# Diagonal squares of the first attention chunk, batched by head groups 0-1, 2-4 and 5-7 instead of 0-1, 2-3 and 4-7

## The chip, the cores and the metric

The kernel runs on one core of one Trainium2 chip. The metric is the time of one execution on the device in microseconds (us). The engines are named as in the profile: PE is the matmul engine (PEld its weight loads), DVE the vector engine, ACT the scalar engine, POOL the GpSimd engine, and SP the engine that issues most of the DMAs.

## What is computed

Two attention layers over 2048 tokens, with 640 channels in 32 heads of 20, whose outputs are laid side by side. Layer A works in four segments of 512 tokens: causal softmax attention inside the segment, mixed by a gate with a read from a memory that the earlier segments have written. Layer B is causal attention with a window of 256 tokens. Of the reference, cut down:

```python
for s in range(4):                       # layer A, segments of L = 512
    p = softmax(qs @ ks.T * scale + causal_mask)
    a_mem = (phi(qs) @ M) / (phi(qs) @ z + 1e-6)
    outs.append(g * a_mem + (1 - g) * (p @ vs))
    M, z = M + phi(ks).T @ vs, z + phi(ks).sum()
# layer B: p = softmax(q @ k.T * scale, where 0 <= i - j < 256);  p @ v
out = concat([A @ wo_A, B @ wo_B])
```

The change lies in segment 0 of layer A, where the memory is still empty.

## The kernel before

**Chunks and groups.** The work is cut into eight chunks of 512 tokens, A0, B0, A1, B1 and so on. The 32 heads form 8 groups of 4 heads. The projections of a chunk are done in five pieces of 128 channels (`qk_job`): piece m gives the q or k of group m (four heads of 20 rows, on partitions 0, 32, 64 and 96), and in the 12 left-over rows of each 32 a part of the heads of groups 5 to 7. Groups 5 to 7 are put together by DMA: when the last piece is there, `regroup` (line 429) stores the left-over rows to DRAM (four DMAs at line 436) and loads them back into place (four DMAs at line 444, one for each head of a group), for k and for q. So groups 0 to 4 can be scored as soon as their piece is done, and groups 5 to 7 only when these DMAs have landed.

**Score batches.** `batches` (line 1091) writes the list of score batches, in the order in which they are issued. For a chunk of A, a group has two strip batches (called a and b here, `BANKS_A`): the scores of 128 keys against all queries from the 65th of that key tile on. What is missing on the diagonal are squares of 64 queries by 64 keys, four for each group. They are batched over several groups, by `SQUARES0` for the first chunk and `SQUARES` for the others: `(g0, ng)` is a batch of the squares of groups g0 to g0 + ng - 1, put right behind the two strip batches of group g0. In this text A3a is the first strip batch of group 3, and S23 the batch of the squares of groups 2 and 3. `score_batch` (line 729) does a batch: its matmuls (line 741; 8 in a strip batch, 16 for each group in a squares batch) into two PSUM tiles `sc`, of which there are three in turn (`NSC`), two exponentials on ACT (line 757) that write two of ten `pt` tiles, and the masks: on POOL for strips (line 796), on DVE for squares (line 774).

**After the scores.** When all batches of a group are there, `av` (line 801) multiplies the `pt` tiles with v: 32 matmuls at line 810. It is called AV3 here for group 3. Then come a transpose on DVE (line 866), which frees the PSUM bank, the reciprocal (891) and the scaling on POOL (901). A `pt` tile is free again when AV of all groups in it has run. The squares take v from a second copy `vS`, which two DMAs for each half of the heads make from `vA` (line 684); its second half serves groups 4 to 7.

**What sets the order.** The kernel writes its instructions in one fixed order for each engine. The order comes from a planner in the kernel (`Flow`, line 63), which charges each piece of work with a written-in cost and puts next what its model says is ready. [...] When a batch is moved, the planner replaces everything behind it anew.

**Around the change** PE also has the projections of A0 (weights `wk_A`, `wq_A`, `wv_A`) and of B0 (`wBk`, `wBq`, `wBv`), all by the helper `wide` (line 853): 5 matmuls of 512 columns for a q or k piece, 5 of 320 columns for a tile of v. DVE evicts them (lines 484, 659 and 664). From each pair of k pieces of A0 come the features phi(k) (`phi`, line 495: ACT line 504, DVE lines 519 and 525); `phi_k` (line 565) stores each piece (`scr_pk`, line 578) and, after the fifth, loads all of them back by a transposing DMA (`pkT`, line 573). SP issues all of these DMAs in its one order. The regroup in `regroup`:

```python
self.nc.sync.dma_start(out=scratch[...], in_=dst[HD * j + DH:HD * j + HD, 0:self.KT, ...])   # line 436
...
self.nc.sync.dma_start(out=dst[HD * j:HD * j + DH, self.KT:G, ...], in_=scratch[...])        # line 444
```

Of the kernel before, what the change touches and what calls it, by code (L numbers as in the profile page):

```python
# [40 lines left out]
SH = P // 2  # L41
XC = SH + L

SQUARES = [(0, 4), (4, 4)]
SQUARES0 = [(0, 2), (2, 2), (4, 4)]
BANKS_A = [[(0, 0), (3, 448)], [(1, 0), (2, 320)]]

STRETCH = 10240.0 / 3.0
# [160 lines left out]
class _K:  # L209
# [881 lines left out]
    def batches(self, chunks):  # L1091

        out = []
        near = lambda n: ("near", 0, n)
        far = lambda n: ("far", P + SH, n)
        for n, (kind, c) in enumerate(chunks):
            if kind == "A":  # L1100
                for g0, ng in SQUARES0 if c == 0 else SQUARES:
                    for g in range(g0, g0 + ng):
                        for ent in BANKS_A:
                            out.append([n, [(g, ("a", kt), P * kt + SH, L - P * kt - SH, c0)
                                            for kt, c0 in ent], [("part", c0, SH) for _, c0 in ent], []])
                        if g == g0:
                            out.append([n, [(g0 + x, ("st"[kt % 2], kt), P * kt, SH,
                                             P * x + SH * (kt // 2))
                                            for x in range(ng) for kt in range(LT)],
                                        [("ends", 1, P * ng)], []])  # L1110
                        out[-1][3].append(g)
                continue

            def ends(g, qt, c0):
                return [(g, ("l", qt + 1), P * qt + SH, SH, c0),
                        (g, ("u", qt - 2), P * qt, SH, c0)]
            if n == len(chunks) - 1:
                for qt in range(LT):
                    for g0 in (0, 2, 4, 6):
                        ent = []  # L1120
                        for x in range(2):
                            ent += [(g0 + x, ("f", qt), P * qt, P, 256 * x),
                                    (g0 + x, ("f", qt - 1), P * qt, P, 256 * x + P)]
                        out.append([n, ent, [near(2), far(2)], []])
                        if g0 == 2:
                            out.append([n, [e for g in range(G) for e in ends(g, qt, SH * g)],
                                        [("ends", 0, L)], [(qt, 0)]])
                    out[-1][3].append((qt, 4))
                continue
            for g0 in range(0, G, 2):  # L1130
                for g in (g0, g0 + 1):
                    ent = [(g, ("f", 0), 0, 2 * P, 0), (g, ("f", 3), 3 * P, P, 2 * P)]
                    if c > 0:
                        ent.append((g, ("f", -1), 0, P, 3 * P))
                    out.append([n, ent, [near(2), far(2 if c else 1)], []])
                    out.append([n, [(g, ("f", 1), P, 2 * P, 0), (g, ("f", 2), 2 * P, 2 * P, 2 * P)],
                                [near(2), far(2)], []])
                    if g == g0:
                        out.append([n, [e for x in range(2) for qt in range(LT)
                                        for e in ends(g0 + x, qt, 256 * x + SH * qt)],  # L1140
                                    [("ends", 0, L)], [g0]])
                out[-1][3].append(g0 + 1)
        return out
# [433 lines left out]
```

## Time and profile before

| what | value |
|---|---|
| median of three runs | 336.32 us (334.82 to 336.74) |
| the profiled execution, its own time | 337.27 us |
| its span, first to last instruction | 335.5 us |
| mean granted clock of PE in it | 0.995 |
| PE busy, share of the span | 94% |
| ACT busy | 90% |
| DVE busy | 79% |
| POOL busy | 76% |

All views are of the profiled execution. The page gives busy shares of the whole span and of 40 equal slices of 8.4 us each. The timeline lists instructions by start time: start, duration, engine, line, operation, result and operands, shape, count, and in brackets the idle time before them with what ended it. The table by stretches gives the length, the busy time of each engine, the granted clock of PE (1.00 is full rate) and the busy share of the DMA engines. SPq is SP's queue of DMA issues.

### The profile page before, as it was taken

The numbers are of one execution on the slowest core, as the hardware profiler recorded it, in microseconds if no ns is written. First come the engines' busy times: TensorE is split into PE (matmuls) and PEld (weight loads), VectorE is DVE, ScalarE is ACT, GpSimd is POOL, SyncE is SP. The second block draws the span as 40 slices with busy tenths as digits, with TensorE's granted clock in tenths as the row PEclk, the third lists the DMA queues.
The fourth block names the chain that finished last, engine by engine and source line by source line (L and its number), as shares of the span: only waits on it lengthen the run. The fifth ranks groups of instructions, "written<-read, shape, count | busy, mean of one in ns | idle before, by whom it ended". The sixth has DMA issues, their size and how long they took to land.

```text
span 335.5 us, 15797 instructions
## 1 busy us (share of the span) xinstructions
PE 317.0 (94%) x6581; PEld 174.8 (52%) x6617; DVE 264.7 (79%) x555; ACT 303.3 (90%) x333; POOL 255.2 (76%) x648
## 2 busy tenths in 40 slices
PE   7899899999899999989999999999999999999996
PEld 2445355545554445455654445555554445666674
DVE  6878467689987899998877899997767889967553
ACT  2899589999899999999999999999999999999861
POOL 8466268898676979986875969997775979987850
PEclk9999799999999999999999999999999999999999
DMA  7966726674566655054598436133674045787862
GB/s 201 388 223 137 172 56 190 163 169 135 139 164 168 148 129 169 3 134 73 122 205 204 98 79 177 31 81 65 135 186 106 9 111 162 162 179 149 171 143 99
DMA packets 76260, 47.28 MB, mean 141 GB/s; under 512 B 48381, under 2 KB 73181, under 8 KB 76189
## 3 DMA queue, kind: packets, MB, share of 16 engines
q1 hardware_dynamic: 75325, 45.46, 55.3%
q8 instruction: 51, 0.84, 1.1%
q10 hardware_dynamic: 864, 0.82, 0.8%
q14 instruction: 20, 0.16, 0.2%
HBM read 17.62 MB, written 16.96 MB: 103 GB/s over the span
## 4 chain that ended last, share of the span: by engine, by line
PE 59%; DVE 16%; POOL 9%; ACT 7%; issue 4%; DMA 2%; SPq 2%; DVEq 0%; ACTq 0%; POOLq 0%
PE m L853 37%; PE sc L741 11%; PE m L810 7%; ACT pt L757 7%; POOL pt L796 5%; DVE pt L774 3%; DVE tt L866 3%; PE m L831 2%; POOL u L901 2%; DMA beta<-in_A_beta_dram 1%; DVE vA L659 1%; DVE kA L484 1%; POOL o L901 1%; SPq L444 1%; DVE pq L525 1%
## 5 line engine op out<-in xcount | busy, mean ns | idle before, releaser
L757 ACT ACTIVATE pt<-sc 128x1024 bf16<-128x1024 f32 (+2 forms) x306 | 285.0, 1013 | 15.8 <-PE sc L741 13.8
L796 POOL TENSOR_SCALAR_AFFINE_SELECT pt<-pt 128x128 bf16<-128x128 bf16 (+1 forms) x512 | 176.3, 372 | 65.8 <-ACT pt L757 61.1
L866 DVE STREAM_TRANSPOSE tt<-m 128x512 f32<-128x512 f32 x88 | 61.3, 710 | 22.7 <-PE m L810 11.0
L901 POOL TENSOR_TENSOR o<-tt,rr 128x320 bf16<-128x320 f32 x64 | 47.7, 746 | 4.2 <-DVE rr L891 4.2
L853 PEld LDWEIGHTS <-xT 128*128 128x128 bf16 x350 | 32.0, 97 | 24.2 <-issue 12.1
L741 PE MATMUL sc<-qB,kB 20*64 20x64 bf16 (+2 forms) x1728 | 38.4, 218 | 0.6 <-ACT pt L757 0.2
L774 DVE TENSOR_TENSOR pt<-pt,ends 128x1024 bf16<-128x1024 bf16 (+1 forms) x50 | 36.0, 734 | 0.0
L741 PE MATMUL sc<-qA,kA 20*64 20x64 bf16 (+4 forms) x1024 | 34.2, 238 | 1.9 <-DMA qA<-scr_qA 1.1
L741 PEld LDWEIGHTS <-kB 20*64 20x64 bf16 (+1 forms) x1728 | 21.6, 98 | 22.3 <-issue 20.8
L1010 DVE CAST ot<-m 128x320 bf16<-128x320 f32 x56 | 26.8, 485 | 7.5 <-PE m L853 7.3
L853 PEld LDWEIGHTS <-oT 128*128 128x128 bf16 x280 | 24.7, 97 | 11.8 <-issue 1.5
L853 PE MATMUL m<-wBv,xT 128*128 128x320 bf16 x160 | 26.9, 300 | 2.4 <-DVE tt L866 2.3
L853 PE MATMUL m<-wv_A,xT 128*128 128x320 bf16 x160 | 26.0, 300 | 2.4 <-DVE vA L659 1.7
L853 PE MATMUL m<-xT,wBq 128*128 128x512 bf16 x94 | 26.8, 391 | 0.9 <-DVE tt L866 0.4
L853 PE MATMUL m<-xT,wBk 128*128 128x512 bf16 x86 | 25.9, 388 | 0.7
L853 PE MATMUL m<-xT,wk_A 128*128 128x512 bf16 x94 | 25.2, 387 | 1.3 <-DVE qA L484 0.7
L853 PE MATMUL m<-xT,wq_A 128*128 128x512 bf16 x90 | 25.0, 381 | 1.3 <-DVE vA L659 0.9
L741 PEld LDWEIGHTS <-kA 20*128 20x128 bf16 (+1 forms) x1024 | 14.0, 97 | 23.4 <-issue 22.5
L810 PE MATMUL m<-pt,vA 128*32 128x192 bf16 (+3 forms) x512 | 23.6, 276 | 0.0
L853 PE MATMUL m<-wo_A,oT 128*128 128x320 bf16 x140 | 22.8, 300 | 0.4 <-DVE vA L659 0.3
L484 DVE CAST kB<-m 128x512 bf16<-128x512 f32 x20 | 13.8, 692 | 9.5 <-PE m L853 9.3
L484 DVE CAST qB<-m 128x512 bf16<-128x512 f32 x20 | 13.8, 689 | 7.7 <-PE m L853 7.7
(107 smaller groups left out, 412.5 us busy)
## 6 DMA issues: line engine op xcount, KB each, us to landing
scr_o<-o SPq DMA_DIRECT2D x28, 160.0 KB
out_dram<-ot SPq DMA_DIRECT2D x28, 160.0 KB
xT<-in_B_x_dram SPq DMA_DIRECT2D x8, 288.0 KB
xT<-in_A_x_dram SPq DMA_DIRECT2D x8, 256.0 KB
scr_pk<-e SPq DMA_DIRECT2D x15, 128.0 KB
scr_kA<-kA SPq DMA_DIRECT2D x16, 60.0 KB
scr_qA<-qA SPq DMA_DIRECT2D x16, 60.0 KB
kA<-scr_kA SPq DMA_DIRECT2D x16, 60.0 KB
```

Source lines behind the costliest of these rows:

```text
L444: self.nc.sync.dma_start(out=dst[HD * j:HD * j + DH, self.KT:G, at:at + L], in_=scratch[:, :].rearrange("(g j d) s -> j d g s", j=4, d=DH)[j])
L484: nc.vector.tensor_copy(out=dst[:, m, at:at + L], in_=ps[:, :])
L741: nc.tensor.matmul(ps[j // 2][h0:h1, j % 2, c0:c0 + nq], lhsT=k[rows, g, k0:k0 + h1 - h0], rhs=q[rows, g, q0:q0 + nq], start=True, stop=Tr ...
L757: nc.scalar.activation(out=pt[:, :, lo:hi], in_=ps[i][:, :, lo:hi], func=ACT.Exp, scale=self.scale)
L774: nc.vector.tensor_tensor(out=blk, in0=blk, in1=self.ends[:, c0, :].unsqueeze(1).unsqueeze(1) .to_broadcast([P, 2, n // SH, SH]), op=ALU.mult)
L796: nc.gpsimd.affine_select(out=blk, in_=blk, pattern=pat, compare_op=ALU.is_ge, fill=self.zero, base=base, channel_multiplier=mul)
L810: nc.tensor.matmul(O[HD * j:HD * j + HD, q0:q0 + nq], lhsT=v[:, VS * h:VS * h + HD], rhs=pts[j // 2][:, j % 2, c0:c0 + nq], start=(n_ == 0 ...
L831: nc.tensor.matmul(O[HD * j:HD * j + HD, o0:o0 + nq], lhsT=v[:, VS * h:VS * h + HD], rhs=pts[j // 2][:, j % 2, c0:c0 + nq], start=(n_ == 0 ...
L853: self.nc.tensor.matmul(ps[:, 0:n], lhsT=lhsT, rhs=rhs, start=start, stop=stop)
L866: self.nc.vector.transpose(out=tt[:], in_=O[:, :])
L901: nc.gpsimd.tensor_tensor(out=to[:] if add_to else to, in0=a, in1=b, op=ALU.mult)
L1010: nc.vector.tensor_copy(out=ot[:, 320 * hf:320 * hf + 320], in_=ps[:, 0:320])
```

## The change

The tuple of a squares batch gets a third number, `at`, which says behind the strips of which of its groups the batch is put. It is 0 everywhere, so each batch still stands behind the strips of its first group. The batches of the first chunk become groups 0-1, 2-4 and 5-7. Those of the other chunks stay.

```diff
-SQUARES = [(0, 4), (4, 4)]
-SQUARES0 = [(0, 2), (2, 2), (4, 4)]
+SQUARES = [(0, 4, 0), (4, 4, 0)]
+SQUARES0 = [(0, 2, 0), (2, 3, 0), (5, 3, 0)]
...
-                for g0, ng in SQUARES0 if c == 0 else SQUARES:
+                for g0, ng, at in SQUARES0 if c == 0 else SQUARES:
                     for g in range(g0, g0 + ng):
...
-                        if g == g0:
+                        if g == g0 + at:
                             out.append([n, [(g0 + x, ("st"[kt % 2], kt), P * kt, SH,
                                              P * x + SH * (kt // 2))
                                             for x in range(ng) for kt in range(LT)],
                                         [("ends", 1, P * ng)], []])
-                        out[-1][3].append(g)
+                        if g >= g0 + at:
+                            out[-1][3].extend(range(g0 if g == g0 + at else g, g + 1))
```

The list of batches in the first chunk was A0a A0b S01 A1a A1b A2a A2b S23 A3a A3b A4a A4b S4567 A5a A5b A6a A6b A7a A7b. It becomes A0a A0b S01 A1a A1b A2a A2b S234 A3a A3b A4a A4b A5a A5b S567 A6a A6b A7a A7b. The orders of the two kernels are the same on each engine up to S23 or S234, and again from the first score batches of B0 on (some 57 us into the profiled execution); only `pt` tile numbers differ there. On PE, in order, with the number of matmuls:

```
before, from the fourth wBk matmul on:
wBk 4, S23 32, wBk 1, wBq 3, A3a 8, wBq 2, wv_A 5, A3b 8, AV2, wv_A 5, A4a 8, wv_A 10, A4b 8, AV3,
wBk 5, S4567 64, wBq 5, wBk 2, A5a 8, wBk 3, wBq 4, A5b 8, wBq 1, wBv 10, AV4, A6a 8, AV5, wBv 5,
A6b 8, wBv 5, wBk 4, A7a 8, wBk 1, wBq 5, wBk 1, A7b 8, wBk 4, AV6
after:
wBk 5, S234 48, wBq 5, A3a 8, wv_A 10, A3b 8, wv_A 5, AV2, A4a 8, wv_A 5, wBk 4, A4b 8, wBk 1, AV3,
A5a 8, wBq 5, wBk 3, A5b 8, wBk 2, wBq 5, wBv 5, AV4, S567 48, wBv 8, A6a 8, wBv 7, wBk 2,
A6b 8, wBk 3, AV5, A7a 8, wBq 5, wBk 2, A7b 8, wBk 3, AV6
```

On SP the fifth `scr_pk` store stands ahead of the four loads of k at line 444, no longer between those of k and those of q. The first part of the x of A1 (line 291), which stood right behind the loads of q, now stands behind the transposing load and the two `vS` DMAs. On DVE the two operations of the fifth phi(k) piece (lines 519 and 525) stand ahead of the eviction of the first q piece of B0 and of both masks of S234; before, line 525 stood behind both masks of S23, that eviction and one of `vA`.

## Prediction

> **What bounds the kernel now.** I read the page's first part (PE 94%, ACT 90%), then the slices for the places where both engines pause. There is one after the start, at slices 4 and 5:
>
> ```profile
> PE   7899899999899999989999999999999999999996
> ACT  2899589999899999999999999999999999999861
> PEclk9999799999999999999999999999999999999999
> ```
>
> Slice 5 (33.5 to 42 us) holds ACT at five tenths and the only dip of PE's clock. Elsewhere ACT runs almost without a gap, so a microsecond won or lost here goes to the end. The timeline of PE shows what happens:
>
> ```profile
> 32.61 1.25 PE L853 MATMUL m<-xT,wBk 128*128 128x512 bf16 x4
> 33.80 0.27 PE L741 MATMUL sc<-qA,kA 20*64 20x64 bf16 x16
> 34.58 0.44 PE L741 MATMUL sc<-qA,kA 20*64 20x64 bf16 x2 [0.51 <-DMA qA<-scr_qA]
> 35.39 0.18 PE L741 MATMUL sc<-qA,kA 20*64 20x64 bf16 x1 [0.37 <-DMA qA<-scr_qA]
> 35.80 0.55 PE L741 MATMUL sc<-qA,kA 20*64 20x64 bf16 x45 [0.23 <-DMA qA<-scr_qA]
> ```
>
> S4567 starts at 33.80 with the 16 matmuls of group 4, and those of group 5 wait for the four loads of q until 35.80. The table by stretches, cut where the clock changes, shows the price of that pause:
>
> ```profile
> 32.98:36.39 3.41, 2.17 (x69) 1.21 (x68) 1.42 (x3) 1.34 (x2) 1.91 (x6) 1.00 0.54 162
> 36.39:39.80 3.41, 3.19 (x14) 0.90 (x13) 1.22 (x3) 1.94 (x2) 0.00 (x0) 0.50 0.89 178
> 39.80:43.21 3.41, 3.31 (x31) 1.52 (x24) 2.34 (x5) 3.16 (x4) 1.22 (x5) 1.00 0.72 173
> ```
>
> For 3.41 us behind the pause the granted clock is 0.50. ACT has nothing meanwhile:
>
> ```profile
> 36.40 1.94 ACT L757 ACTIVATE pt<-sc 128x1024 bf16<-128x1024 f32 x2 [2.08 <-PE sc L741]
> 40.05 3.88 ACT L757 ACTIVATE pt<-sc 128x1024 bf16<-128x1024 f32 x4 [1.71 <-PE sc L741]
> 45.26 14.31 ACT L757 ACTIVATE pt<-sc 128x1024 bf16<-128x1024 f32 x16 [1.33 <-PE sc L741]
> ```
>
> From 45.26 on ACT is the bound: sixteen exponentials without a gap. So the question is when A6a's exponential, the one at 45.26, can start. The chain of waits says what the pause waits for, SP's queue:
>
> ```profile
> 31.77 0.36 SPq L578
> ...
> 32.23 0.30 SPq L444
> ...
> 33.36 2.40 DMA qA<-scr_qA
> ```
>
> The last load of q is issued at 33.36 and is there at 35.76.
>
> **Work added or removed: none.** The squares of groups 2 to 7 are 96 matmuls either way. ACT had two exponentials of 512 columns (0.594 us) and two of 1024 (1.031): 3.25 us. It gets four of 768, which last 0.815 in B0: 3.26. The DVE masks have no row for 768 columns; they lie between 0.42 (512) and 0.68 (1024), and I take the middle, so that four cost what the two pairs did. Only places move.
>
> **Ahead of the pause.** PE's projections are the same before the first matmul that needs a load (10 wBk, 5 wBq, 20 wv_A), so are four strip batches, AV2 and AV3. S234 has 16 matmuls more than S23 (0.26 us for 32, so 0.13 more), and the 16 of group 4 at 33.80 are gone from the pause. I carried the after order forward from 24.2 us with the rows' durations: 0.216 us for each 512-column matmul, 0.156 for 320 columns, 0.33 for a strip batch, 0.67 for AV, an eviction of 0.69 or 0.49. S234's exponentials are 0.22 longer each and start 0.2 later, so ACT's A4b ends at about 35.3 instead of 34.3; its slack was the 2.08 us of idle time. PE reaches A5a at 33.7 (no more waiting for banks than before) to 34.1, and finds q absent as S4567 did.
>
> **The landing.** SP now issues the fifth pk store ahead of k's four loads. It waits for DVE's line 525. That ran at 28.42 to 28.96 behind two masks and two evictions; now it stands right behind the eviction of the first k piece of B0 (25.82 to 26.51), so I put its end at 27.2. SP gets to it at 28.96 as its queue stands, so it costs no wait, k's loads move by 0.46 us, and q's loads keep their place at 32.23. Landing: 35.8, taken unchanged (35.4 if the store, out of the way earlier, frees the rings; 36.2 if k's shift is passed on). Behind q the transposing load comes at 33.80 instead of 35.73, because its last store is now three microseconds older, and `vS` at 36.9 instead of 38.80.
>
> **The clock.** The stretch at half rate is worth: from the end of S4567 (36.35) to the start of A5a (39.33 to 39.39) lie 7 wide matmuls and a gap of 0.22; at full rate 7 x 0.216 = 1.5. So 1.5 us are lost. What was streamed in the stretch before it? By the planner's own count (columns / 2.4, squares at half): wBk from 32.98 to 33.80, 0.83 us; S4567, 512 / 2.4 = 0.21; the first wBq, 0.04. [...] After: the same stretch holds A4b (0.21), the last wBk (0.21), AV3 (1280 / 2.4 = 0.53), A5a (0.21) and wBq from 36.05 (0.34): 1.50, a share of 0.44 if PE arrives at 34.0. If it arrives at 33.7 the poorest position of a stretch (32.4 to 35.8) holds 0.28. So the pause is as long, but what lies beside it is denser: AV3 and two strips stand where five projections and late squares stood. I take it that the clock holds, with the other case kept as a rival, since one row of the trace gives the bound from one side only: the next poorest stretch I found without a drop, 145.62 to 149.03, had PE busy for 2.49 us against 2.17.
>
> [...]
>
> **Behind the pause.** At full rate: A5a 35.8 to 36.05, wBq 5 and wBk 3 (1.73) to 37.8, A5b to 38.1, wBk 2 and wBq 5 (1.51) to 39.6, wBv 5 to 40.4, AV4 to 41.1, S567 (0.5) to 41.6, wBv 8 to 42.7 or 42.9, A6a to 43.2. A6a's exponential follows after 0.2 to 0.45 (0.45 in the trace): 43.4 to 43.65, with S567's done at 43.3. From there ACT has the same 8 exponentials to B0 and is fed in time (A6b 45.0, A7a 46.7, A7b 48.6). Against 45.26 that is 1.6 to 1.85 earlier. Of it 1.5 is the clock. The rest, 0.1 to 0.35, is that wBv 10 stood in a piece ahead of AV4 while ACT had nothing, and that a part of S4567's exponential (group 4) was done ahead of the pause, in S234. If the clock drops as before, the same count with eight matmuls at 0.43 gives A6a's exponential at 45.05: 0.2 earlier.
>
> **Sum** against the profiled execution (span 335.5, its own time 337.27): -1.4 for the clock (1.5, less what the later exponentials of A4b eat) and -0.2 for the order, -1.6. Nothing behind 57 us moves but in time, and ACT's gapless run carries it to the end. That execution is 0.95 above the median of 336.32; the difference is taken to carry over. **Forecast: 334.7 us**, about what the quickest of the three runs had (334.82), which may be one without the drop.
>
> **Rivals.**
>
> *The half-rate stretch stays* (chance 0.30). For it: the pause is as long, and an arrival at 33.7 makes a stretch of 0.28. Against it: the share at 34.0 is 0.44. The time is 336.3 - 0.2 = 336.1.
>
> *AV4 waits for vS* (0.13). AV4 comes at 40.4 instead of 43.75. `vS` was issued at 38.80 to 40.10; at q's pace (2.4 us) it lands at 42.5 there. If SP's transposing load does not move up (it waits for the slowest pk store), vS comes at 42.5 again and the gain is returned: PE stands 1.5 to 2 us, ACT with it, as S567 and A6a need `pt` tiles that only AV4 frees. The time is 336.4. Against it: the pk store is issued three microseconds earlier.
>
> *Slower: SP stands at the fifth pk store* (0.10). Before, k's loads did not depend on DVE's fifth phi piece; now they and q's do. From an end of line 525 later than 28.96 each microsecond delays the landing by one. If that operation ends at 31 (DVE's first phi operations or ACT's exponential come late), the landing is at 37.8: PE stands 3.8 us, the clock surely drops, and the time is 336.3 + 2.0 - 0.2 = 338.1.
>
> *The change does nothing that can be told* belongs to the second: the squares are 0.5 us of ACT that only change sides.
>
> **How the numbers follow.** Forecast 0.46, half rate 0.30, vS 0.13, SP 0.10, and 0.01 left. The forecast's own range is 333.6 (landing at 35.4, nothing waits) to 335.6 (landing at 36.2, A6a's exponential late). The range over all cases: down to 333.6, up to 337.2, which holds the first three and leaves most of the last out. A measurement tells about 0.5% (1.7 us) from no change; the forecast lies at -0.48%, so its chance is split nearly in halves. Faster by more 0.29, within 0.59 (the other half and the two rivals in the middle), slower 0.12 (SP's wait, and a late landing with a drop).
>
> **What would show it.** The stretch behind the pause at a granted clock of 1.00; the first waiting matmul is A5a, with its last wait ended at 35.4 to 36.2; ACT's idle time ahead of A5a down from 2.08 to some 0.9, and one idle time of about 1.5 ahead of S567; A6a's exponential at 43.4 to 43.7; the transposing load issued near 33.8. It is wrong if SP stands at line 578 behind DVE, if AV4 waits for vS, or if the clock shows 0.50 again.

## The result, and the profile after

| | before | changed |
|---|---|---|
| median | 336.53 us (4 runs, 334.82 to 337.59) | 340.75 us (4 runs, 340.11 to 341.22) |
| profiled execution | 337.27 us | 341.08 us |
| its span | 335.5 us | 339.4 us |

The ratio is 1.0129, with a 95% interval of 1.0082 to 1.0176: the change made the kernel slower by 1.3%, outside the range forecast and on the other side. (All ratios here leave out executions over 1.5% above the quickest of their kernel, so a ratio can differ from that of two medians.)

The page of the changed kernel, second part, shows where. The slices are 8.5 us now:

```profile
PE   8999399999999999989999999999999999999996
ACT  2899359999999999999999999989999999999961
PEclk9999699999999999999999999999999999999999
```

The one slice that had ACT at five tenths before has three, the next one five, and PE itself is at three tenths. The timeline of PE has the reason:

```profile
33.24 0.59 PE L810 MATMUL m<-pt,vA 128*32 128x448 bf16 x12
33.66 0.20 PE L810 MATMUL m<-pt,vS 128*32 128x64 bf16 x3
39.58 0.63 PE L810 MATMUL m<-pt,vS 128*32 128x64 bf16 x13 [5.72 <-DMA vS<-vA]
39.98 0.29 PE L810 MATMUL m<-pt,vA 128*32 128x64 bf16 x4
40.20 0.61 PE L741 MATMUL sc<-qA,kA 20*128 20x448 bf16 x8
```

This is AV3. Three of its 16 matmuls on squares run, and the fourth waits 5.72 us for a DMA into `vS`. Only then comes A5a (40.20), and no wait for q, for which S4567 had waited, is listed ahead of it. SP's part of the timeline says which DMA:

```profile
28.42 1.18 SPq L578 DMA_DIRECT2D scr_pk<-e  x2
29.66 1.72 SPq L444 DMA_DIRECT2D kA<-scr_kA  x4
31.47 2.40 SPq L444 DMA_DIRECT2D qA<-scr_qA  x4
33.92 2.54 SPq L573 DMA_TRANSPOSE pkT<-scr_pk  x1
36.57 1.31 SPq L684 DMA_DIRECT2D vS<-vA  x2
```

The only `vS` DMAs under way are those of the second half, groups 4 to 7. They are issued from 36.57 on, behind the transposing load, and the second one lands at 39.83. Group 3 belongs to the first half, whose copy was made long before. In the kernel before AV3 ran at 31.94, and these DMAs were issued at 38.80: it did not wait for them.

The table by stretches, cut where the clock changes (the granted clock is the figure behind the five engines), shows the second half of the price:

```profile
33.57:36.98 3.41, 0.29 (x15) 0.11 (x3) 0.47 (x1) 1.47 (x2) 1.57 (x6) 1.00 0.73 163
36.98:40.39 3.41, 0.76 (x21) 0.48 (x25) 0.08 (x1) 0.00 (x0) 0.00 (x0) 0.50 1.01 238
40.39:43.81 3.42, 3.20 (x15) 1.03 (x8) 1.58 (x3) 1.94 (x2) 1.77 (x5) 0.50 0.30 103
43.81:47.22 3.41, 3.31 (x34) 1.46 (x36) 1.79 (x3) 1.94 (x2) 1.09 (x4) 1.00 0.00 0
```

PE is at half rate for two stretches (6.83 us at 0.50). In the first it stands almost all the time and loses little; in the second it works. ACT's timeline gives the sum:

```profile
40.93 1.94 ACT L757 ACTIVATE pt<-sc 128x1024 bf16<-128x1024 f32 x2 [5.89 <-PE sc L741]
44.58 1.94 ACT L757 ACTIVATE pt<-sc 128x1024 bf16<-128x1024 f32 x2 [1.71 <-PE sc L741]
48.25 1.51 ACT L757 ACTIVATE pt<-sc 128x768 bf16<-128x768 f32 x2 [1.73 <-PE sc L741]
50.09 12.54 ACT L757 ACTIVATE pt<-sc 128x1024 bf16<-128x1024 f32 x14 [0.33 <-PE m L853]
```

A6a's exponential starts at 50.09, against 45.26 before: 4.8 us late. The span ends 3.9 late; where the 0.9 between is given back was not traced.

**Theory 1.** AV3 waits for data that it does not use. `av` reads 32 columns of weights for each head, though a head has 21 (`VS`). For the fourth head of group 3 (number 15) these are columns 315 to 346 of `vS`. The second half's DMAs write from column 336 on. The two overlap in 11 columns, whose products land in rows that nobody reads. That fits the row above, in which the fourth matmul is the one that waits. By this theory AV3 waits for the DMAs whenever they stand ahead of it in the program, whatever the data are needed for. Before, A4b alone stood between the last piece of wv_A, from which `vS` is copied, and AV3, and the planner wrote AV3 first. In the changed kernel four wBk matmuls, A4b and one more wBk stand there, by then the modelled time of the DMAs has come, and they are written first. **Rival 2:** `vS` is late because SP issues the transposing load ahead of it, and the wait would only move to another place. **Rival 3:** the regroup of q is what sets the time.

### The profile page after: what moved, and what is told of

Its sections match the earlier page's. It is cut to its first block, busy times and chain, and to the rows that moved or that the text cites. A ratio compares the mean times of both kernels' runs of the same rounds, so it can differ in the third digit from the quotient of the medians.

```text
span 339.4 us, 15791 instructions
## 1 busy us (share of the span) xinstructions
PE 316.9 (93%) x6580; PEld 174.7 (51%) x6617; DVE 264.0 (78%) x555; ACT 303.0 (89%) x333; POOL 255.8 (75%) x648
## 4 chain that ended last, share of the span: by engine, by line
PE 57%; DVE 16%; POOL 8%; ACT 7%; issue 5%; SPq 3%; DMA 3%; DVEq 0%; POOLq 0%; ACTq 0%
PE m L853 36%; PE sc L741 11%; PE m L810 7%; ACT pt L757 7%; POOL pt L796 5%; DVE tt L866 3%; DVE pt L774 3%; PE m L831 2%; DVE kA L484 2%; POOL u L901 2%; DMA beta<-in_A_beta_dram 1%; DVE pq L525 1%; SPq L444 1%; DVE pq L519 1%; DVE ot L1010 1%
## 5 line engine op out<-in xcount | busy, mean ns | idle before, releaser
L774 DVE TENSOR_TENSOR pt<-pt,ends 128x1024 bf16<-128x1024 bf16 (+2 forms) x50 | 35.6, 725 | 0.0
L741 PE MATMUL sc<-qA,kA 20*64 20x64 bf16 (+4 forms) x1024 | 33.4, 238 | 0.5
L853 PE MATMUL m<-wo_B,oT 128*128 128x320 bf16 x120 | 19.6, 300 | 0.3 <-DVE ot L1010 0.3
```

What stands on the lines that cost most here:

```text
L741: nc.tensor.matmul(ps[j // 2][h0:h1, j % 2, c0:c0 + nq], lhsT=k[rows, g, k0:k0 + h1 - h0], rhs=q[rows, g, q0:q0 + nq], start=True, stop=Tr ...
L774: nc.vector.tensor_tensor(out=blk, in0=blk, in1=self.ends[:, c0, :].unsqueeze(1).unsqueeze(1) .to_broadcast([P, 2, n // SH, SH]), op=ALU.mult)
L853: self.nc.tensor.matmul(ps[:, 0:n], lhsT=lhsT, rhs=rhs, start=start, stop=stop)
```

## The experiments

**The DMAs behind AV3 in the program** (`e1_hold`). All engines, SP among them, keep the order of the changed kernel:

```diff
+        if n == 0 and half == 1:
+            f.blocked.append((t, self.known("av3"), lambda t0: go()))
+        else:
+            f.at(t, go)          # in v_squares
...
+            if n == 0 and g == 3:
+                self.mark(f.pe - 200.0, "av3")
             O, bi = self.av(     # in one_group
```

> The changed kernel, with the two DMAs of the second vS half written into the program behind AV3 instead of ahead of it, and the order of the instructions on each engine unchanged (SP's too): only the wait of AV3's fourth square matmul on these DMAs goes. Theory 1 (AV3 waits for data that it does not use: its fourth head reads 32 columns of vS, 315 to 346, and the DMAs write from 336 on): the wait of 5.72 us in AV3 is gone, PE passes to A5a and waits there for q until 35.5 to 36.2, vS (issued at 36.6, landed at 39.8) is there before AV4 needs it, and the time is 334.5 to 336.5. Rival 2 (vS is late because SP issues the transposing load ahead of it, and groups 4 to 7 need it anyway): the wait moves to AV4 or A5a, and the time stays at 339 to 341. Rival 3 (the regroup of q lands late): A5a waits beyond 38, and the time stays above 338.5.

Measured: 1.0001 of before (0.9968 to 1.0035); 12 runs from 335.33 to 340.80, with a median of 339.05 beside 337.91 for before on the same chip. That is above the 334.5 to 336.5 expected, in part because before was higher here too (336.53 in the first measurement). PE's timeline of its profiled execution (335.33 us, span 333.6; the lines of the code stand 3 lower):

```profile
33.70 0.29 PE L813 MATMUL m<-pt,vS 128*32 128x64 bf16 x16
33.81 0.20 PE L813 MATMUL m<-pt,vA 128*32 128x64 bf16 x4
34.81 0.49 PE L744 MATMUL sc<-qA,kA 20*128 20x448 bf16 x2 [0.79 <-DMA qA<-scr_qA]
35.66 0.48 PE L744 MATMUL sc<-qA,kA 20*128 20x448 bf16 x6 [0.36 <-DMA qA<-scr_qA]
36.07 1.25 PE L856 MATMUL m<-xT,wBq 128*128 128x512 bf16 x4
```

The 16 matmuls run through, and A5a waits for q, as the prediction had it. `vS` is issued as late as in the changed kernel (36.81), yet AV4, which needs it, runs at 40.70 without a wait. The stretch behind the pause has the full clock:

```profile
36.39:39.80 3.41, 3.36 (x23) 1.36 (x23) 1.38 (x2) 3.18 (x4) 1.38 (x7) 1.00 0.99 206
```

So the wait makes the loss, or nearly all of it: with the same order on every engine and without the wait, the ratio tells no loss, though up to 0.35% stays possible, and the median is 1.1 us above before's. `vS` comes as late as before and A5a has its q at 35.66, so rival 2 falls as the cause, and so does rival 3.

**The same kernel once more** (`e8_hold_again`).

> A second look at the changed kernel with the second vS half behind AV3. Its twelve times spread over 335.3 to 340.8, while its profile (span 333.6) had the full clock throughout. If the spread comes from the time at which q lands and from the half clock behind it, a profile in the upper half shows q later than 36.5 and a clock of 0.50 behind it, and one in the lower half neither; AV3 waits for vS in neither.

One run, 336.67 us, span 333.8: the full clock again, A5a's q there at about 36.2, no wait in AV3. It fell in the lower half of the spread and showed what was expected of that half. For the upper half the mean granted clock of the twelve executions of `e1_hold` has the answer: the five from 335.33 to 337.62 us have 1.00, the three from 338.84 to 339.52 have 0.995, the mean of the profile of before, which has 3.41 us at 0.50, and the four from 340.26 on have 0.99, that of the changed kernel's, which has 6.83 us. That q was late in those is not recorded.

**`vS` as two tiles** (`e2_split` for the changed kernel, `e3_before_split` for the one before). The overlap itself is gone:

```diff
-        self.vS = big.tile([P, LT, VW], BF16, name="vS")
+        self.vS = [big.tile([P, LT, VW - 16 * VS], BF16, name="vS%d" % i) for i in range(2)]
...
-                return self.vS[:, 2 * (u % 2) + u // 2, :]
+                return self.vS[g // 4][:, 2 * (u % 2) + u // 2, :]
```

> The changed kernel with vS as two tiles, one for each half of the heads, each with its own 12 spare columns; the order on each engine is unchanged but for one more memset on POOL. AV3 of no chunk can wait for the second half. Theory 1: as the kernel with the DMAs behind AV3, within 0.5 us, or up to 0.5 us less since AV3 of A1 waits for it too in all the other kernels: 334.0 to 336.5. Rival 2: 339 to 341.

> The kernel before with vS as two tiles. Here AV3 of A0 stands ahead of the DMAs in the program and never waited for them. Theory 1: 336.0 to 336.6, at most 0.5 us less than before (AV3 of A1). The difference between this and the changed kernel with two tiles is what the change itself is worth; by the prediction -0.2 to -1.6 us, by a rival in which the change is bad of itself +1 us or more.

Measured: 1.0001 (0.9972 to 1.0031) for the changed kernel, 0.9989 (0.9962 to 1.0015) for the one before, on one chip. A second way to remove the wait gives the same as the first, and the kernel before, which had no wait, gains nothing that can be told. That the loss is there on this chip too when the wait stays is shown by `e4_vs_first` below. It also follows that AV3 of A1, which stands behind such DMAs in both kernels, costs nothing: the profiles of both list no wait there. The median of the first (338.52, beside 337.91 of before) lies above the 334.0 to 336.5 expected, and so does that of the second (337.88, expected 336.0 to 336.6): on this chip all of them ran higher. The profiled execution of `e2_split` is a long one (340.60) and shows one way to such a time:

```profile
34.53 0.20 PE L810 MATMUL m<-pt,vA 128*32 128x64 bf16 x4
36.72 1.74 PE L741 MATMUL sc<-qA,kA 20*128 20x448 bf16 x8 [1.98 <-DMA qA<-scr_qA]
38.40 0.61 PE L853 MATMUL m<-xT,wBq 128*128 128x512 bf16 x1
```

AV3 does not wait, but SP issues q's loads from 34.28 on instead of 31.47, A5a gets its last q near 38.2, and the clock is at 0.50 from 36.45 to 43.27. The pause ahead of A5a is 3.5 us long here and 1.7 in `e1_hold`, with the same order of work. But the length alone does not decide: the clock fell 1.7 us after PE had stopped (34.73), when the pause was about as long as the whole of that in `e1_hold`.

The places of the falls tell more. The clock is at 0.50 from 36.39 to 39.80 in the kernel before, from 36.98 to 43.81 in the changed one and from 36.45 to 43.27 in `e2_split`: for 3.41, 6.83 and 6.82 us. In the 3.41 us ahead of its fall (32.98 to 36.39) the kernel before had PE busy for 2.17 us; in the same 3.41 us `e1_hold` had PE busy for 2.25, and its clock held. `e3_before_split` has the same order on PE as the kernel before and as long a pause (33.88 to 35.87), but there the clock held, in the 3.41 us that end inside the pause and in those that begin there:

```profile
31.43:34.84 3.41, 2.72 (x64) 1.32 (x63) 2.21 (x5) 2.97 (x4) 2.59 (x9) 1.00 0.60 170
34.84:38.25 3.41, 2.70 (x61) 1.35 (x61) 0.62 (x2) 1.79 (x2) 0.87 (x2) 1.00 1.07 229
```

Ahead of the fall in `e2_split` PE was busy for 1.74 of 3.50 us (33.00 to 36.50). PE's busy time does not tell the two cases apart, for `e7_split_q_first` had PE busy for 1.91 of 3.50 us (34.00 to 37.50), a smaller share than the 2.17 of 3.41 ahead of the fall in the kernel before, and its clock held. Why the clock fell in one execution and held in another of the same order is not shown.

The mean clocks of all executions say that the changed order is not the safer one once its wait is gone. On this chip 7 of 24 executions of `e1_hold` and `e2_split` had the full clock and 8 had 0.99 or less; of before and `e3_before_split` 21 of 41 had the full clock and one had 0.99.

**The transposing load behind `vS`** (`e4_vs_first`). The wait stays, SP's order is changed:

```diff
-        gate = self.known("dm", c - 1) if c > 0 else (lambda: 0.0)
+        gate = self.known("dm", c - 1) if c > 0 else self.known("vS")   # set when vS is issued
...
```

> The changed kernel with the transposing load behind the second vS pair on SP instead of ahead of it (the first two parts of x now stand ahead of vS, and the planner moves some work of B0 on PE). AV3's wait stays in the program. Theory 1: vS is issued at about 35 instead of 36.6 and lands at 37.5 to 38.5, so AV3's wait shrinks by 1.5 to 2.5 us, and the time is 338 to 339.5. Rival 2: the wait is gone, 335.5 to 337. Rival 3: no change, 340.5 to 341.

Measured: 1.0102 (1.0075 to 1.0128). The PE timeline:

```profile
33.81 0.20 PE L812 MATMUL m<-pt,vS 128*32 128x64 bf16 x3
38.43 0.24 PE L812 MATMUL m<-pt,vS 128*32 128x64 bf16 x4 [4.42 <-DMA vS<-vA]
39.09 0.34 PE L812 MATMUL m<-pt,vS 128*32 128x64 bf16 x9 [0.42 <-DMA vS<-vA]
```

`vS` is issued 1.3 us earlier (35.31) and the wait is 0.9 us shorter (4.42 and 0.42 instead of 5.72), less than expected; most of it stays, and the time with it (median 341.27, all six executions from 340.60 on). The transposing load set some of the wait's length, not its being there.

**The wait put into the kernel before** (`e5_before_now`). The batches are the old ones:

```diff
+        if n == 0 and half == 1:
+            go()
+        else:
+            f.at(t, go)          # in v_squares
```

> The kernel before, with the two DMAs of the second vS half written into the program as soon as the last tile of vA is, which is ahead of AV3 (on SP they now stand right behind the loads of q and ahead of the transposing load; PE's order is that of before up to A5b). So the wait is put into the kernel that did not have it, without the change of the batches. Theory 1: AV3's fourth square matmul, which stood at 32.4 without a wait, waits until vS has landed, at about 36.5 to 37.5; the clock falls behind it; q is there by then, so S4567 no longer waits; the time is 1 to 3 us above before. Rival (the loss belongs to the new batches, the wait only takes the place of the one for q): within 0.5 us of before.

Measured: 1.0126 (1.0083 to 1.0168), a loss like that of the changed kernel without its change (4.2 us between the medians, more than the 1 to 3 expected). PE's timeline:

```profile
32.49 0.20 PE L813 MATMUL m<-pt,vS 128*32 128x64 bf16 x3
36.58 0.64 PE L813 MATMUL m<-pt,vS 128*32 128x64 bf16 x13 [3.88 <-DMA vS<-vA]
```

Here too the fourth matmul waits, and the clock is at 0.50 from 36.4 to 39.8. (The planner also moves work behind A5b in this kernel, up to some 180 us, so the size of the loss is not that of the wait alone.)

**SP's order and the landing of q** (`e6_before_q_first`, and with two `vS` tiles `e10_before_split_q_first`; for the changed batches with two tiles `e7_split_q_first` and, once more, `e9_split_q_first_again`). The last two phi(k) stores are held until the loads of q are issued:

```diff
...
+            if n == 0 and m >= 3:
+                f.blocked.append((t, self.known("spread"), lambda t0: store()))
+            else:
+                f.at(t, store)   # in phi_k; "spread" is set behind q's loads
```

> The kernel before, with the fourth and fifth phi(k) stores behind the regroup's loads on SP. Theory (the pause ahead of groups 5 to 7 is set by SP's issue order, and half a clock follows from it): the last load of q is issued about 0.9 us earlier and lands near 34.8 instead of 35.8; S4567 waits about 1 us less, the clock is less often at half, and the time is 0.8 to 2.5 us below before. Rival (the landing is set by the DMA engines): no change within 0.5 us.

> The changed batches with vS as two tiles, and the fourth and fifth phi(k) stores behind the regroup's loads on SP. Theory 1 with the landing set by SP: no wait in AV3, A5a's wait ends near 34.7, so the pause is under 1 us and the clock stays; 1.0 to 3 us below before, that is 334 to 336.5. If the changed batches are worse of themselves: above the same edit of the kernel before by more than 0.5 us.

> The changed batches with vS in two tiles and the last two phi(k) stores behind the regroup's loads, once more, on the same chip as the same two edits of the old batches. If the change of the batches is worth something of itself once no wait stands in its way: 0.2 to 1.5 us below the other kernel of this pair, 335 to 337. If it is worth nothing: within 0.5 us of it.

> The old batches (0-1, 2-3, 4-7) with vS in two tiles and the last two phi(k) stores behind the regroup's loads. As the kernel before with the stores moved alone, ratio 0.998 to before, since AV3 of A0 did not wait there; any distance to the pair kernel is the change of the batches alone.

In all four the planner also moves other work, from some 40 to 180 us, so this is not a change of SP's order alone. Measured: `e6` 0.9983 (0.9951 to 1.0015), no change that can be told. Its loads of q are issued from 30.70 instead of 32.23, yet the squares of groups 5 to 7 run from 35.32 to 36.31 with a wait ahead of them, so q is there no earlier: that SP's issue time sets the landing does not hold in this execution. In the profile of `e10`, with the same edit of SP's order, PE never waits for q (span 332.6). What sets the landing stays open.

The changed batches with both edits give 0.9954 (0.9926 to 0.9983) and again 0.9943 (0.9905 to 0.9981), with medians of 335.70 and 335.69 beside 337.54 and 337.32: half a per cent below before, and the best of all kernels here. The number expected of `e7` came, but not for the reason given: A5a's last wait ended at 36.40, not near 34.7, and the pause was 2.2 us long. The old batches with the same edits (`e10`) give 0.9963 (0.9930 to 0.9996), median 336.68.

What comes with the moved stores is the clock: 45 of the 48 executions of these four had it in full (0.998 or more), of before on the same two chips 21 of 46. By which path is not shown, since q came no earlier in the profiles of `e6`, `e7` and `e9`. Among executions at the full clock the old batches gain nothing (medians 336.71 and 336.46, before 336.19 and 336.54). The new batches lie below the old ones by 1.0 us in both pairs (335.70 beside 336.73 of `e6`, which has one `vS` tile, and 335.69 beside 336.68), as expected of `e9` if they are worth something of themselves; each pair alone does not tell this from nothing. ACT's timeline of `e9` shows one place:

```profile
36.66 1.94 ACT L762 ACTIVATE pt<-sc 128x1024 bf16<-128x1024 f32 x2 [1.55 <-PE sc L746]
38.83 3.35 ACT L762 ACTIVATE pt<-sc 128x1024 bf16<-128x1024 f32 x4 [0.23 <-PE sc L746]
42.41 16.23 ACT L762 ACTIVATE pt<-sc 128x1024 bf16<-128x1024 f32 x18 [0.23 <-ACT pt L762]
```

A5a comes 0.4 us later than in `e1_hold` (36.66 against 36.25), but A5b and S567 follow each other, where `e1_hold` had 1.73 us of idle time ahead of S567, and A6a is at 42.41 instead of 43.94. With the stores moved, `vS` stands ahead of the transposing load on SP, and the planner puts AV4, and S567 behind it, two pieces earlier (39.19 instead of 40.70). This does not account for the gain: the span of this execution, the longest of its twelve, is 334.8, 1.2 us longer than that of `e1_hold`, so the lead of 1.5 us at A6a was lost again further on.

## Why the prediction was wrong

**The step that failed** is "Ahead of the pause", where PE's work up to A5a was taken over with the waits that it had before: "PE reaches A5a at 33.7 ... to 34.1, and finds q absent". AV3 had moved behind the `vS` DMAs in the program, which made a wait of 5.72 us inside AV3. I had listed which data each piece of work uses, and by that AV3 uses none of the second half. `vS` appeared as a rival, but at AV4, at a price of 1.5 to 2 us, and with the argument that it would be issued earlier; it was (36.57), and that did not help AV3, which wanted it at 33.86. The rival that ended on the slower side named SP at the fifth pk store, and that was not it: line 525 ended at 27.11 (predicted 27.2), and q's loads were issued from 31.47.

**Point by point.**

- *Work added or removed: none.* Right. ACT's four exponentials of 768 columns cost what was reckoned (0.805 to 0.810 us each, reckoned at 0.815); the masks took 0.55 to 0.71, at the middle taken (0.55) or above it.
- *PE at the pause between 33.7 and 34.1, q there at 35.8.* Right once the wait is gone: AV3 ends near 34.0 and q's last wait at 35.66 in `e1_hold`, near 36.2 in `e8_hold_again`. SP's queue, the transposing load at 33.92 and `vS` at 36.57, came as reckoned (33.80 and 36.9).
- *The clock holds.* Not so in general. `e1_hold` and `e8_hold_again` had the full clock, `e2_split`, with q at 38.2, had 6.82 us at 0.50. For an arrival at 34.0 the prediction weighed what PE streams beside the pause (a share of 0.44, and 0.28 at 33.7). No run shows that such a share decides: `e3_before_split` kept the full clock in the order in which the kernel before lost it, and `e7_split_q_first` kept it with PE busy for 1.91 of 3.50 us. The kernel before also runs at full rate in 35 of 75 executions on three chips, and the changed order without its wait in 7 of 24. The -1.4 was a difference between two executions, not between two programs.
- *The order is worth -0.2.* The two profiles without a drop have spans of 333.6 (`e1_hold`) and 333.8 (`e3_before_split`); A6a's exponential starts at 43.94 against 43.69 there. The ratios of 1.0001, 1.0001 and 0.9989 do not tell it from nothing. With the stores moved both pairs have the new batches 1.0 us lower by the medians, and behind some 55 us the two of a pair have one order; but the intervals of 0.9943 and 0.9963 overlap, so this gain is likely and not shown.
- *The size of the loss.* Of the 6.15 us between `e1_hold` and the changed kernel at A6a's exponential (43.94 to 50.09), 4.7 lie between the ends of A5a (36.07 to 40.75), which is the wait, and 1.5 between A5a and A5b (1.84 us long there, 3.32 here), which is the half clock. The spans differ by 5.8. Against the profile of before, which had 3.41 us at half rate itself, 3.9 are left.

The clock of the changed kernel fell 3.1 us into a gap of 5.72 us. That of the kernel before fell after a pause of 2.0 us with no gap above 0.51 us in it, and the same order with two `vS` tiles did not lose it (`e3_before_split`), so a pause of 2.0 us can come with a fall here and without one.

## What to carry to other kernels

When a planner or a scheduler moves work, ask of each moved instruction not only which data it uses but which region it touches, and what now stands ahead of it in the program that touches the same region: a read widened for convenience can wait for a write that has nothing to do with it. Such a wait is tested by turning round the two in the program while every engine keeps its order, or by giving the halves tiles of their own. A gain that is read off one execution's clock belongs to that execution until others show it, and the mean granted clock of many executions shows it without a profile.

## What the runs showed of the hardware

PE's granted clock fell to 0.50 some 3.1 us after PE had stopped in the changed kernel (33.86 to 36.98), 1.7 us after in `e2_split` (34.73 to 36.45), and was at 0.50 for 6.83 us in the first and 6.82 in the second (3.41 in the kernel before); in the first 3.41 of its 6.83 us the changed kernel's PE was busy for 0.76. At the pause looked at here the clock fell behind 3.41 us with PE busy for 2.17 (kernel before) and held behind the same 3.41 us with 2.25 (`e1_hold`), and it also held with PE busy for 1.91 of 3.50 us (`e7_split_q_first`); what decides is not shown.

The last load of q was there at 35.7 us in `e1_hold` and at 38.2 in `e2_split`, with the same order on SP; some 1.8 us of this are its later issue (the four loads had been issued by 33.91 and by 35.71). Loads of q issued 1.5 us earlier (from 30.70 instead of 32.23) were there no earlier in the profile of `e6_before_q_first`, where the matmuls of wBq behind them start at 36.31, beside 36.28 before; in that of `e10_before_split_q_first` PE lists no wait for them.

The executions of `e1_hold` spread over 5.5 us, in the order of their mean clocks. The clock is not all of it: those of `e9_split_q_first_again`, all at the full clock, spread over 3.2 us.
